# First block of a fused attention and MLP kernel: V weights loaded in two halves, tile 0 multiplied by the first half early, transposes placed inside matmul groups

## Chip, cores and metric

The kernel runs on one core of one Trainium2 chip. The metric is the device time of one execution in microseconds (us), measured on the core. The profile is one execution. Its span, from the first to the last instruction, is some 1.8 us shorter than the time.

## The reference

```python
x = A_x                                             # 1 x 2048 x 1024, bf16
h = x + attention(layernorm(x), wqkv, wo)           # 32 heads of 32, causal window of 256
h2 = h + silu(layernorm(h) @ w1) @ w2               # 1024 -> 3584 -> 1024
```

The layer norm has no weights. The argument concerns only the first 512 rows: their norm, their transposition, and their V = layernorm(x) @ wqkv[:, 2048:3072].

## The kernel before

The 2048 rows are worked on in four blocks of 512, a block in four tiles of 128 rows. At the start each tile of x is loaded, normed on VectorE and turned (transposed). TensorE turns tiles 0 to 2, and ScalarE copies the result out of PSUM. Tile 3 is turned by a DMA transpose from SBUF to SBUF. Then each tile is multiplied by the V weights in two groups of eight matmuls: `v_group(0, j, c)` is tile j times columns c*512 and up, and ScalarE evicts it. Behind these eight groups come the Q and K groups, which need all four turned tiles.

```python
for queue, c0 in ((nc.sync, 0), (nc.scalar, 512)):
    queue.dma_start(out=x_ring[0][:, c0:c0 + 512], in_=x2d[0:P, c0:c0 + 512])
load_x(0, 1)
for queue, k0 in ((nc.scalar, 0), (nc.sync, 4)):
    queue.dma_start(out=wv[:, k0:k0 + 4, 0:512], in_=wqkv_v[:, k0:k0 + 4, 2 * D:2 * D + 512])
# ... cut: one activation ...
load_x(0, 2)
load_wqkv(2 * D + 512)          # second V weights, 1 MB, rows of 1 KB
load_x(0, 3)
load_wqkv(0)                    # first Q weights
# ... cut: identity, constants ...
for i in range(11):             # warm-up matmuls on zeros
    nc.tensor.matmul(o_ps[i % 2][:].rearrange("p a b -> p (a b)"), lhsT=warm[:, 0, 0:P], rhs=warm[:, 0, :], start=True, stop=True)
# ... cut ...
ln_first(x_ring[0], ...)        # norm of tile 0, in quarters; tile 1's first statistics go in it
turn_first(x_ring[0], lnT_b[0], 0)
# ... cut: statistics of tile 1, in quarters ...
ln_first(x_ring[1], ...)
v_group(0, 0, 0, act, turn_1)   # tile 1's eight transposes ahead of its last matmul
ln_whole(x_ring[2], st, rs, 2)
v_group(0, 1, 0, act)
ln_whole(x_ring[3], st, rs, 3)
ln_transpose(x_ring[3], lnT_b[0], 3)      # DMA transpose of tile 3
for c0 in (D, 512, D + 512):
    load_wqkv(c0)                         # other Q and K weights, on the same queue
v_group(0, 0, 1, act)
turn_first(x_ring[2], lnT_b[0], 2)
v_group(0, 1, 1, act)
v_group(0, 2, 0, act); v_group(0, 2, 1, act)
# ... cut: one activation ...
v_group(0, 3, 0, act); v_group(0, 3, 1, act)
```

The softmax here doesn't subtract the row's maximum and nothing guards it: scores larger than these inputs give would overflow.

## Time and profile before

| what | before | where it is read |
|---|---|---|
| time, median of 6 runs | 697.04 us (696.97 to 698.03) | the runs |
| first V matmul | 6.89 us | timeline |
| tile 3 landed / its statistics begin | 11.9 / 12.70 us | DMA view, timeline |
| tile 3's DMA transpose, issue to landing | 15.93 + 3.2 us | DMA view |
| first Q/K matmul | 22.68 us | timeline |

In a timeline or chain, the first number is the start in us from the span's start and the second the length. In brackets stands how long the engine was idle before, and what ended that. Engines: PE is TensorE, PEld its weight load, DVE VectorE, ACT ScalarE, SPq the queue that issues DMAs. L numbers are lines of the kernel, and the change shifts them: L203 becomes L205, L251 L253, L261 L266.

### The profile page before, as it was taken

The numbers are of one execution on the slowest core, as the hardware profiler recorded it, in microseconds if no ns is written. First come the engines' busy times: TensorE is split into PE (matmuls) and PEld (weight loads), VectorE is DVE, ScalarE is ACT, GpSimd is POOL, SyncE is SP. The second block draws the span as 40 slices with busy tenths as digits, with TensorE's granted clock in tenths as the row PEclk, the third lists the DMA queues.
The fourth block names the chain that finished last, engine by engine and source line by source line (L and its number), as shares of the span: only waits on it lengthen the run. The fifth ranks groups of instructions, "written<-read, shape, count | busy, mean of one in ns | idle before, by whom it ended". The sixth has DMA issues, their size and how long they took to land.

```text
span 695.2 us, 12339 instructions
## 1 busy us (share of the span) xinstructions
PE 690.3 (99%) x5091; PEld 331.7 (48%) x5091; DVE 289.9 (42%) x618; ACT 257.9 (37%) x328; POOL 174.6 (25%) x391
## 2 busy tenths in 40 slices
PE   8999999999999999999999999999999999999998
PEld 3444454555555555544444444444444444444445
DVE  6267646644443448544316133333133251244111
ACT  4326667777777777621310023300033100233000
POOL 1007667777777677500000000000000000000000
PEclk9999999999999999999999999999999999999999
DMA  7832241036240778980023410023300025100110
GB/s 243 256 60 70 40 93 46 17 63 189 71 128 19 215 248 274 190 312 31 31 76 100 106 38 1 1 88 72 83 1 1 13 94 91 45 1 1 30 39 24
DMA packets 76617, 60.84 MB, mean 88 GB/s; under 512 B 50320, under 2 KB 60816, under 8 KB 76560
## 3 DMA queue, kind: packets, MB, share of 16 engines
q1 hardware_dynamic: 75888, 59.39, 31.2%
q8 instruction: 40, 0.66, 0.4%
q10 hardware_dynamic: 672, 0.66, 0.3%
q14 instruction: 17, 0.14, 0.1%
HBM read 39.85 MB, written 8.39 MB: 69 GB/s over the span
## 4 chain that ended last, share of the span: by engine, by line
PE 98%; DVE 1%; DMA 0%; ACT 0%; issue 0%
PE hacc L581 19%; PE hacc L618 17%; PE acc L261 16%; PE acc L618 10%; PE acc L581 9%; PE acc L251 8%; PE acc L280 7%; PE o_ps L352 4%; PE sc L298 3%; PE hacc L280 1%; PE o_ps L367 1%; PE sc L326 1%; DMA r_o<-in_A_x_dram 0%; PE tp L229 0%; DVE r_o L199 0%; DVE ln_st L171 0%
## 5 line engine op out<-in xcount | busy, mean ns | idle before, releaser
L343 POOL TENSOR_SCALAR_AFFINE_SELECT r_e<-r_e 128x256 bf16<-128x256 bf16 (+1 forms) x384 | 171.6, 477 | 116.0 <-ACT r_e L335 64.6
L306 ACT ACTIVATE r_e<-sc 128x1024 bf16<-128x1024 f32 x144 | 139.5, 1021 | 45.1 <-PE sc L298 31.0
L618 PEld LDWEIGHTS <-r_a 128*128 128x128 bf16 x952 | 90.9, 98 | 103.0
L581 PEld LDWEIGHTS <-r_w 128*128 128x128 bf16 x896 | 87.4, 98 | 104.8
L618 PE MATMUL hacc<-r_a 128*128 128x512 bf16 (+2 forms) x616 | 122.5, 360 | 0.0
L581 PE MATMUL hacc<-r_e,r_w 128*128 128x512 bf16 x456 | 100.9, 379 | 0.0
L590 ACT ACTIVATE r_n<-hacc 128x512 f32<-128x512 f32 x30 | 17.9, 597 | 178.9 <-PE hacc L581 178.9
L618 PE MATMUL acc<-r_a 128*128 128x512 bf16 x336 | 74.0, 379 | 0.0
L261 PEld LDWEIGHTS <-r_w 128*128 128x128 bf16 x512 | 46.5, 98 | 57.0 <-issue 7.0
L263 DVE CAST r_a<-acc 128x512 bf16<-128x512 f32 x56 | 38.7, 691 | 72.4 <-PE acc L261 55.7
L261 PE MATMUL acc<-r_t,r_w 128*128 128x512 bf16 x256 | 60.0, 379 | 0.0
L261 PE MATMUL acc<-r_w 128*128 128x512 bf16 x256 | 58.2, 380 | 0.0
L280 PE MATMUL acc<-r_o,r_a 128*128 128x512 bf16 x208 | 49.4, 380 | 0.0
L581 PE MATMUL acc<-r_e,r_w 128*128 128x512 bf16 x216 | 49.1, 379 | 0.0
L352 PEld LDWEIGHTS <-r_e 128*128 128x128 bf16 x1152 | 39.6, 96 | 17.0
L335 ACT ACTIVATE r_e<-sc 128x1024 bf16<-128x1024 f32 x36 | 34.9, 1021 | 21.2 <-PE sc L326 20.1
L352 PE MATMUL o_ps<-r_a,r_e 128*128 128x33 bf16 x1152 | 40.2, 178 | 0.0
L633 DVE SCALAR_TENSOR_TENSOR r_t<-hacc,r_t 128x512 bf16<-128x512 f32 (+2 forms) x22 | 14.0, 636 | 56.8 <-PE hacc L618 56.8
L280 PEld LDWEIGHTS <-r_a 128*128 128x128 bf16 x256 | 23.1, 98 | 29.6 <-issue 5.1
L633 DVE SCALAR_TENSOR_TENSOR r_t<-acc,r_t 128x512 bf16<-128x512 f32 x12 | 8.3, 692 | 64.2 <-PE acc L618 64.2
L591 DVE SCALAR_TENSOR_TENSOR r_a<-r_n,hacc 128x512 bf16<-128x512 f32 x30 | 20.6, 688 | 33.0 <-ACT r_n L590 33.0
L581 PE MATMUL hacc<-r_a,r_w 128*128 128x512 bf16 x144 | 32.9, 379 | 0.0
(75 smaller groups left out, 477.2 us busy)
## 6 DMA issues: line engine op xcount, KB each, us to landing
r_w<-in_B_w_dram SPq DMA_DIRECT2D x8, 896.0 KB, 5.2
r_a<-in_B_w_dram SPq DMA_DIRECT2D x7, 1024.0 KB, 7.7
r_w<-in_A_wqkv_dram SPq DMA_DIRECT2D x5, 1024.0 KB, 9.4
h_dram<-r_t SPq DMA_DIRECT2D x16, 256.0 KB, 3.6
r_t<-h_dram SPq DMA_DIRECT2D x16, 256.0 KB, 2.9
out_dram<-r_t SPq DMA_DIRECT2D x31, 128.0 KB, 1.7
r_o<-in_A_x_dram SPq DMA_DIRECT2D x15, 256.0 KB, 4.1
r_e<-h_dram SPq DMA_DIRECT2D x3, 1024.0 KB, 5.6
```

Source lines behind the costliest of these rows:

```text
L251: nc.tensor.matmul(acc, lhsT=lnT_b[b % 2][:, kt, j * P:(j + 1) * P], rhs=wv[:, kt, c * 512:(c + 1) * 512], start=(kt == 0), stop=(kt == KT ...
L261: nc.tensor.matmul(acc, lhsT=wqk[:, kt, col0:col0 + P], rhs=lnT_b[b % 2][:, kt, :], start=(kt == 0), stop=(kt == KT - 1))
L263: copy(out=(qT, kT)[which][b][:, g, :], in_=acc)
L280: nc.tensor.matmul(acc, lhsT=qT[b][:, g, j * P:(j + 1) * P], rhs=wo[:, g, c * 512:(c + 1) * 512], start=(g == 0), stop=(g == G - 1))
L298: nc.tensor.matmul(sc[hh // 2][:, hh % 2, ch * P:(ch + nq) * P], lhsT=kT[t // 4][r0:r0 + DH, g, (t % 4) * P:(t % 4 + 1) * P], rhs=qT[b][r0 ...
L306: nc.scalar.activation(out=e, in_=sc[pair], func=ACT.Exp, scale=scale)
L335: nc.scalar.activation(out=e, in_=sc[pair], func=ACT.Exp, scale=scale)
L343: nc.gpsimd.affine_select(out=ap, in_=ap, pattern=[[0, 2], [0, n], [sgn, P]], compare_op=ALU.is_ge if upper else ALU.is_gt, fill=0.0, base ...
L352: nc.tensor.matmul(o_ps[pair][:, qt * 2 + hh, 0:VW], lhsT=e_of(i, kind, pair)[:, hh, ch * P:(ch + 1) * P], rhs=v[:, b * 4 + kt, g * 4 + pa ...
L581: nc.tensor.matmul(acc, lhsT=w1[:, kt, ft * P:(ft + 1) * P], rhs=ln2T[b][:, kt, :], start=(kt == 0), stop=(kt == KT - 1))
L618: nc.tensor.matmul(acc[:, 0:c1 - c0], lhsT=gT[:, ft, j * P:(j + 1) * P], rhs=w2[ft // 4][:, ft % 4, c0:c1], start=(ft == 0), stop=(ft == F ...
L633: nc.vector.scalar_tensor_tensor(out=t_out[j % 2][:, c0:c1], in0=acc[:, 0:c1 - c0], scalar=0.5, in1=t_in[j % 2][:, c0:c1], op0=ALU.mult, o ...
```

## The change

The intent is to give TensorE work while it waits for tile 1's norm. The second V weights come in two loads of 256 columns. Tile 0 is multiplied by the first 256 columns right behind its first group, and tile 1's transposes stand between those matmuls. Tile 2's transposes go inside another group. Tiles 2 and 3 are normed by one instruction each, and the first half of tile 3's statistics goes ahead of tile 2's reciprocal.

```diff
-    load_x(0, 2)
-    load_wqkv(2 * D + 512)
+    for j, c0 in ((2, 512), (3, 768)):
+        nc.sync.dma_start(out=wv[:, :, c0:c0 + 256], in_=wqkv_v[:, :, 2 * D + c0:2 * D + c0 + 256])
+        if j == 2:
+            load_x(0, 2)
     load_x(0, 3)
     load_wqkv(0)
-    for i in range(11):
+    for i in range(10):
 ... cut: ln_whole takes half_done and ahead; ln_norm of the whole tile instead of four quarters;
 ... cut: turn_first turns one pair of blocks; v_cols does a group of any width;
 ... cut: turn_at(j, when) puts tile j's pairs ahead of the matmuls numbered in when
-    v_group(0, 0, 0, act, turn_1)
-    ln_whole(x_ring[2], st, rs, 2)
+    v_group(0, 0, 0, act)
+    v_cols(0, 0, 512, 768, act, turn_at(1, (3, 5, 7)))
+    turn_first(x_ring[1], lnT_b[0], 1, 3)
+    half = small.tile([P, 2, 6], F32, name="ln_st", tag="ln_st")
+    ln_whole(x_ring[2], st, rs, 2, None, (x_ring[3], half))
     v_group(0, 1, 0, act)
-    ln_whole(x_ring[3], st, rs, 3)
+    ln_whole(x_ring[3], st, rs, 3, half)
 ... cut: DMA transpose of tile 3 and the next loads, unchanged
-    v_group(0, 0, 1, act)
-    turn_first(x_ring[2], lnT_b[0], 2)
-    v_group(0, 1, 1, act)
+    v_cols(0, 0, 768, 1024, act)
+    v_group(0, 1, 1, act, turn_at(2, (3, 4, 5, 6)))
```

More of the change, by code (lines that the diff above doesn't have):

```diff
@@ L216, in ln_quarter, with ln_whole, turn_first @@
         nc.vector.bn_stats(out=stats[:, c, :], in_=xt[:, c * 256:(c + 1) * 256])
-    def ln_whole(xt, st, rs, j):
-        ln_stats(xt, st, j)
+    def ln_whole(xt, st, rs, j, half_done=None, ahead=None):
+        ln_stats(xt, st, j, half_done)
         nc.scalar.activation(out=rs[:, j:j + 1], in_=st[:, j, 1:2], func=ACT.Sqrt, bias=eps[:], scale=1.0)
+        if ahead is not None:
+            ln_half(*ahead, 0)
         nc.vector.reciprocal(out=rs[:, j:j + 1], in_=rs[:, j:j + 1])
-        for h in range(4):
-            ln_norm(xt[:, h * 256:(h + 1) * 256], st, rs, j)
-    def turn_first(xt, dst, j):
-        for h in range(4):
-            for i in range(2):
-                kt = h * 2 + i
-                nc.tensor.transpose(out=tp_ps[h][:, i * P:(i + 1) * P], in_=xt[:, kt * P:(kt + 1) * P], identity=ident[:])
-            nc.scalar.copy(out=dst[:, h * 2:(h + 1) * 2, j * P:(j + 1) * P],
-                           in_=tp_ps[h][:, 0:256].rearrange("p (k q) -> p k q", q=P))
+        ln_norm(xt, st, rs, j)
+    def turn_first(xt, dst, j, h):
+        for i in range(2):
+            kt = h * 2 + i
+            nc.tensor.transpose(out=tp_ps[h][:, i * P:(i + 1) * P], in_=xt[:, kt * P:(kt + 1) * P], identity=ident[:])
+        nc.scalar.copy(out=dst[:, h * 2:(h + 1) * 2, j * P:(j + 1) * P],
+                       in_=tp_ps[h][:, 0:256].rearrange("p (k q) -> p k q", q=P))
     def ln_tiles(tag):
@@ L244, in next_acc, with v_cols @@
         return acc_banks[acc_n[0] % len(acc_banks)]
-    def v_group(b, j, c, copy, between=None):
-        acc = next_acc()
+    def v_cols(b, j, c0, c1, copy, between=None):
+        acc = next_acc()[:, 0:c1 - c0]
         for kt in range(KT):
@@ L250, in v_group @@
                 between(kt)
-            nc.tensor.matmul(acc, lhsT=lnT_b[b % 2][:, kt, j * P:(j + 1) * P], rhs=wv[:, kt, c * 512:(c + 1) * 512],
+            nc.tensor.matmul(acc, lhsT=lnT_b[b % 2][:, kt, j * P:(j + 1) * P], rhs=wv[:, kt, c0:c1],
                              start=(kt == 0), stop=(kt == KT - 1))
-        copy(out=v[:, b * 4 + j, c * 16:(c + 1) * 16, 0:DH], in_=acc.rearrange("p (h d) -> p h d", d=DH))
+        copy(out=v[:, b * 4 + j, c0 // DH:c1 // DH, 0:DH], in_=acc.rearrange("p (h d) -> p h d", d=DH))
+    def v_group(b, j, c, copy, between=None):
+        v_cols(b, j, c * 512, (c + 1) * 512, copy, between)
     def qk_group(b, which, g, copy, between=None):
@@ L405 @@
     ln_first(x_ring[0], st, rs, 0, halves, lambda: ln_quarter(x_ring[1], quarters, 0))
-    turn_first(x_ring[0], lnT_b[0], 0)
+    for h in range(4):
+        turn_first(x_ring[0], lnT_b[0], 0, h)
     for c in range(1, 4):
@@ L409, with turn_at, between @@
     ln_first(x_ring[1], st, rs, 1, quarters)
-    def turn_1(kt):
-        if kt == 7:
-            turn_first(x_ring[1], lnT_b[0], 1)
-    v_group(0, 0, 0, act, turn_1)
-    ln_whole(x_ring[2], st, rs, 2)
+    def turn_at(j, when):
+        def between(kt):
+            if kt in when:
+                turn_first(x_ring[j], lnT_b[0], j, when.index(kt))
+        return between
+    v_group(0, 0, 0, act)
[3 more added lines that the diff above has]
+    ln_whole(x_ring[2], st, rs, 2, None, (x_ring[3], half))
     v_group(0, 1, 0, act)
-    ln_whole(x_ring[3], st, rs, 3)
+    ln_whole(x_ring[3], st, rs, 3, half)
     ln_transpose(x_ring[3], lnT_b[0], 3)
```

## The prediction

> **What bounds the kernel now.** I read the page's busy row and chain of waits first, then the chain in order of time for the first 30 us, then the timeline of the first 36 us, and last the DMA view in narrow windows, which gives the landing of single transfers. TensorE is busy nearly throughout and the chain is its own:
>
> ```profile
> PE 690.3 (99%) x5091; PEld 331.7 (48%) x5091; DVE 289.9 (42%) x618; ACT 257.9 (37%) x328; POOL 174.6 (25%) x391
> ...
> PE 98%; DVE 1%; DMA 0%; ACT 0%; issue 0%
> ```
>
> So a change to the first block can only pay by what TensorE loses before its first Q/K matmul (22.68 us); everything behind it shifts by as much. The chain in order of time shows what is lost there (start, length, what):
>
> ```profile
> 8.36 0.17 DVE rs_a L211
> 8.53 0.03 issue
> 8.56 0.35 DVE r_o L199
> 8.91 0.05 issue
> 8.96 1.05 PE tp L229 x8
> 10.02 3.67 PE acc L251 x17
> 13.69 0.45 PE tp L229 x8
> 14.13 8.71 PE acc L251 x40
> ```
>
> The eight transposes of tile 1 take 1.05 us because each pair waits for a normed quarter; the eight of tile 2, whose data are ready, take 0.45 us. TensorE also stands idle for 0.39 us before the first. The timeline gives the rest (start, length, engine, line):
>
> ```profile
> 6.89 1.67 PE L251 MATMUL acc<-r_w 128*128 128x512 bf16 x7
> 9.59 1.28 DVE L171 BATCH_NORM_STATS2 ln_st<-r_o 128x6 f32<-128x512 bf16 x2
> 11.67 1.11 DVE L199 TENSOR_SCALAR r_o<-r_o,st_a,rs_a 128x256 bf16<-128x256 bf16 x4
> 12.70 1.28 DVE L171 BATCH_NORM_STATS2 ln_st<-r_o 128x6 f32<-128x512 bf16 x2
> 14.79 1.11 DVE L199 TENSOR_SCALAR r_o<-r_o,st_a,rs_a 128x256 bf16<-128x256 bf16 x4
> 15.93 1.34 SPq L203 DMA_TRANSPOSE r_w<-r_o  x1
> 19.22 3.14 PEld L251 LDWEIGHTS <-r_w 128*128 128x128 bf16 x16 [0.40 <-DMA r_w<-r_o]
> ```
>
> Lost time: from 6.89 to 22.68 are 15.79 us. The work in it is 64 matmuls of 512 columns at 216 ns (13.82) and 16 transposes at 56 ns (0.90), 14.72 together. So 1.07 us is lost, about 1.0 of it at tile 1. At tile 3 the weight load stands 0.40 us, but the 24 matmuls from 13.97 on keep the array until 19.15, so only about 0.1 is lost there. **The ceiling of the change is thus about 1.1 us of 697**, and tile 3's DMA transpose, landing at 19.2, lies hard behind it.
>
> Landings, as issue time plus time to landing: second quarter-load of the first V half 1.72 + 5.8 = 7.5; tile 2 2.19 + 6.0 = 8.2; second V half 2.73 + 8.4 = 11.1; tile 3 and the first Q weights from
>
> ```profile
> r_o<-in_A_x_dram SPq DMA_DIRECT2D x1, 256.0 KB, 8.7
> r_w<-in_A_wqkv_dram SPq DMA_DIRECT2D x1, 1024.0 KB, 10.5
> ```
>
> 3.21 + 8.7 = 11.9 and 4.36 + 10.5 = 14.9. They land in the order of issue, 1 MB in 2.9 us (8.2 to 11.1, about 360 GB/s).
>
> [...] 16 matmuls of 512 columns between 19.22 and 22.68 are 216 ns each, and tile 2's transposes 55 ns. [...] here the warm-up matmuls start 0.43 us apart (half speed) up to the last at about 5.80, and the matmul behind it starts at 6.09, so the release came at about 5.95. [...] the new half loads have rows of exactly 512 B, which no transfer of this size in the trace has. [...] four quarters of a norm take 1.11 us, and the later norms of a whole 128x1024 tile 0.54 to 0.58 us.
>
> **The change part by part.**
> - *One warm-up matmul less.* The array is free at 5.80 instead of 6.09; the first transpose waits for the norm that ends at 5.94. The first V matmul follows the first copy of tile 0 and the last transpose pair at 6.77, so it stays at 6.89. Worth 0.
> - *V weights 512 to 1023 as two loads, tile 2 between.* The same bytes in another order: first part 7.5 + 1.45 = 8.95, tile 2 9.7 (was 8.2), second part 11.15, tile 3 unchanged 11.9.
> - *Tile 0 times columns 512 to 767 before tile 1 is needed.* The first V group runs through and ends its streaming at 6.89 + 8 x 0.216 = 8.62. The new half group waits for its weights until 8.97: a DMA wait of 0.35 us takes the place of the one on the norm (0.39). Then 8 x 0.109 = 0.87 and the transposes 8 x 0.056 = 0.45 among them; the quarters are normed at 8.91, 9.17, 9.43, 9.68, each before its pair is due (9.30, 9.63, 9.96, 10.18). Tile 1's first group starts at 10.29. Before it started at 10.07 without the half group (0.87). Gain here 0.65.
> - *Tile 1 group, second half group, tile 1's second group with tile 2's transposes in it.* 1.73 + 0.87 + 1.73 + 0.45 puts the end at 15.07, against 15.70 before: 0.63 ahead. Tile 2 must be normed when its first pair is due at 12.89 + 0.65 = 13.54.
> - *VectorE.* Tile 2's statistics start at 9.71 instead of 9.59 (landing), aggregate done at 11.23. Then comes the first half of tile 3's statistics, ahead of tile 2's reciprocal, so it waits for tile 3's landing: 11.92 to 12.55. Reciprocal and whole norm: 12.59 to 13.35, later than now (12.78) but before 13.54. Tile 3: second half 13.37 to 14.01, aggregate 14.25, square root on ScalarE 14.29 to 14.58, reciprocal, norm 14.81 to 15.37. Now it ends at 15.90: **0.53 earlier**. The DMA transpose is issued at 15.40 and, with the same 3.27 us (15.93 to 19.2), lands at 18.67.
> - *ScalarE.* Its order puts tile 3's square root before the second half group's eviction and tile 2's copies. Eviction from 14.49, first copy 14.76 to 15.15, and with the 0.10 us from copy to matmul that tile 0 shows (6.79 to 6.89) tile 2's V groups start at 15.25, not 15.07: 0.18 us of new stall.
> - *Sum.* 15.25 + 16 x 0.216 = 18.70 for tile 3's first matmul; its data are there at 18.67. Then 16 x 0.216 = 3.45: first Q/K matmul at 22.15 instead of 22.68. **Gain 0.53 us**: 0.65 won at tile 1, 0.1 of tile 3's stall removed, 0.18 lost to the copies, the remainder rounding. Behind it the program is the same and TensorE-bound, and its loads are issued some 0.5 us earlier too. 697.03 - 0.53 = 696.5.
>
> **The rivals.**
> 1. *Tile 3's landing decides.* Its half statistics now stand before tile 2's reciprocal, so tile 2 and tile 3 both hang on the landing at 11.9. If rows of 512 B cost 10%, the two half loads take 0.3 us longer, tile 3 lands at 12.2, tile 2 is normed at 13.65, tile 3's transpose lands at 18.97 and the gain falls to about 0.23 (696.8). With 20% nothing is left (697.1). For it: the DMA engines are at 0.93 to 1.09 share all the time to 14 us, so nothing hides a slower transfer. [...]
> 2. *The whole loss is removed* because the first part lands earlier than I think and tile 3 is no limit. Then 1.07 us and 696.0. Against: bytes in the queue are the same up to tile 3, and the DMA transpose has a fixed 3.27 us; 18.67 alone keeps it at about 0.55.
> 3. [...] Then the first V group runs at half speed, 1.7 us more, of which the waits at 8.95 absorb 0.35: about 698. [...]
> 4. *The gain is given back later* by a load or mask. Against: the page shows no TensorE wait but the two of this block.
>
> **Range and chances.** The ceiling at 696.0 needs rival 2; the VectorE chain makes less than 0.65 likely. On the other side a somewhat slower first transfer takes off 0.1 to 0.3. The three runs before lie within 0.07 us, so the range is mine, not noise: 696.5, from 696.2 to 697.0. 2% is 13.9 us, more than ten times the ceiling: faster 0.01, same 0.98, slower 0.01.
>
> **What would show it right or wrong.** In the profile after: (a) first V group unbroken from about 6.89; (b) the half group starting at 8.9 to 9.1 with a wait on the V weights; more than 9.2 means slow 512 B rows; (c) tile 1's transposes in pairs within 0.11 us, no wait on the norm; (d) VectorE idle for about 0.7 us before tile 3's first half statistics, until the landing near 11.9; (e) whole norms of 0.54 to 0.58 us; (f) tile 2's V groups starting near 15.25, behind the copies; (g) DMA transpose issued near 15.4, landed near 18.7; (h) first Q/K matmul near 22.15. The prediction is wrong if (h) and the end do not shift alike, if the half group's matmuls are slower than 109 ns, or if the first V group runs at half clock.

With them go the opening sentence of rival 3, which said that the clock is released later for want of the eleventh warm-up matmul, the argument against that rival, and the last argument against rival 1. The sum came to a first Q/K matmul at 22.15 us instead of 22.68, a gain of 0.53 us, and so to 696.5 us. The spacings in it are in the trace of the kernel before: 216 ns for 512 columns and 56 ns for 128 in this block, and 109 ns for the 28 matmuls of 256 columns at L618. The "release" is the step in that trace from matmuls 0.43 us apart to 0.216.

## The result

The changed kernel takes **698.60 us** as the median of 6 runs: 697.10, 697.32, 698.42, 698.77, 698.80 and 699.03. The kernel before takes 697.04 us. The ratio is 1.0014 (95% interval 1.0001 to 1.0027). Such a ratio is the mean time of one kernel's runs over that of the other's of the same rounds, so it is not quite the ratio of the medians. The prediction was 696.5 us, from 696.2 to 697.0. The runs are slower instead of faster, and they fall into two sorts, two near 697.2 and four between 698.4 and 699.0.

The profiled run (698.80 us) is of the slow sort. In its chain in order of time (start, length, what), the part that answers to the one shown of before reads:

```profile
4.50 8.09 DMA r_o<-in_A_x_dram
12.58 0.02 issue
12.61 0.69 DVE ln_st L173
...
15.35 0.56 DVE r_o L201
15.91 0.02 issue
15.93 5.13 DMA r_w<-r_o
21.06 0.05 issue
21.10 3.63 PE acc L253 x16
24.73 5.40 PE acc L266 x25
```

Before, TensorE's own matmuls filled this stretch. Now the chain hangs on tile 3. Its load lands at 12.6 us (11.9 before). Its DMA transpose is issued at 15.93, exactly as before, but takes 5.13 us instead of 3.2. TensorE then does tile 3's 16 matmuls from 21.10 instead of 19.22. TensorE's waits in the changed kernel (us in total, times, longest):

```profile
PE acc L253 <- DMA r_w<-r_o: 1.8, 1, 1.8
PE o_ps L169 <- DVE r_e L164: 1.6, 1, 1.6
PE acc L253 <- DMA r_w<-in_A_wqkv_dram: 0.6, 1, 0.6
```

The third line is the half group waiting for its weights, and the first is tile 3. The second, before the warm-up, is there in both kernels. The first Q/K matmul is at 24.57 us instead of 22.68. These 1.89 us answer to the 1.76 us by which this run is longer than the median of before, so all of the loss lies in the first block.

Two more readings. The windows view gives, behind the engines, the granted clock, the DMA engines' busy share and the GB/s. Before:

```profile
6.50:8.50 2.00, 2.00 (x12) 0.83 (x11) 1.60 (x6) 1.40 (x5) 0.00 (x0) 1.00 1.08 363
9.50:11.50 2.00, 2.00 (x13) 1.00 (x13) 1.60 (x5) 1.77 (x6) 0.00 (x0) 1.00 1.08 361
```

After, in the same stretches, while the half loads run:

```profile
6.50:8.50 2.00, 2.00 (x14) 1.01 (x13) 1.60 (x6) 1.46 (x5) 0.00 (x0) 1.00 1.17 313
9.50:11.50 2.00, 2.00 (x20) 1.55 (x20) 1.54 (x4) 1.43 (x5) 0.00 (x0) 1.00 1.18 310
```

The DMA engines are busier and move 14% less. And in the timeline, VectorE and then TensorE wait for what comes late:

```profile
12.61 0.69 DVE L173 BATCH_NORM_STATS2 ln_st<-r_o 128x6 f32<-128x512 bf16 x1 [0.95 <-DMA r_o<-in_A_x_dram]
...
14.00 0.11 PEld L231 LDWEIGHTS <-r_o 128*128 128x128 bf16 x2 [0.33 <-DVE r_o L201]
...
15.70 0.11 PEld L253 LDWEIGHTS <-r_w 128*128 128x128 bf16 x2 [0.50 <-ACT r_w L232]
```

VectorE stands 0.95 us for tile 3's landing with tile 2's reciprocal queued behind it. So the weight load stands 0.33 us before tile 2's transposes and 0.50 us before its V groups. These are not yet losses of the array, which still has matmuls queued: by the starts of the matmuls it loses less than 0.03 us at the first and 0.17 us at the second.

**What is between the transpose and its landing?** The DMA view of 18.9 to 20 us of the changed kernel shows, beside the data queue, one packet of another queue:

```profile
q1 hardware_dynamic: 209, 0.21, 80.9%
q8 instruction: 1, 0.02, 5.2%
```

The page of either kernel lists 40 such packets, 0.66 MB, so 16 KB each. Whose instructions they bring the page does not say, but the trace of the changed kernel lets one count: from the start of one such packet to the start of the next, TensorE starts 188 to 320 instructions (matmuls and weight loads), 256 in the median and 255.9 in the mean, while the medians of VectorE, ScalarE and GpSimd are 14, 16 and 18. So I take the queue q8 to bring TensorE's instructions, some 256 a packet. Whether this costs anything here is what the experiments ask.

The packet records of the trace give the times. The first fetch starts at 19.01 us and takes 0.92 us. The transpose's 1024 data packets end at 19.02. Of the 32 packets of 4 bytes behind them (semaphore updates, I think; the records do not name them), 30 end by 18.70, and the last two start at 19.92 and 19.93, when the fetch is nearly over. In the kernel before, the last of the 32 ends at 18.71, and the first fetch starts only at 23.95 us.

### The profile page after: what moved, and what is told of

It is laid out like the page before. It is cut to its first block, busy times and chain, and to the rows that moved or that the text cites. A ratio compares the mean times of both kernels' runs of the same rounds, so it can differ in the third digit from the quotient of the medians.

```text
span 697.0 us, 12347 instructions
## 1 busy us (share of the span) xinstructions
PE 690.2 (99%) x5098; PEld 332.2 (48%) x5098; DVE 288.9 (41%) x612; ACT 258.3 (37%) x329; POOL 175.2 (25%) x391
## 4 chain that ended last, share of the span: by engine, by line
PE 97%; DMA 2%; SPq 0%; DVE 0%; issue 0%; ACT 0%
PE hacc L628 21%; PE hacc L591 18%; PE acc L266 16%; PE acc L591 10%; PE acc L628 7%; PE acc L285 7%; PE acc L253 7%; PE o_ps L357 4%; PE sc L303 3%; PE hacc L285 1%; PE o_ps L372 1%; DMA r_o<-in_A_x_dram 1%; PE sc L331 1%; DMA r_w<-r_o 1%; SPq L138 0%; DVE ln_st L173 0%
## 5 line engine op out<-in xcount | busy, mean ns | idle before, releaser
L628 PE MATMUL hacc<-r_a 128*128 128x512 bf16 (+2 forms) x728 | 146.5, 363 | 0.0
L591 PE MATMUL hacc<-r_e,r_w 128*128 128x512 bf16 x432 | 95.7, 379 | 0.0
L600 ACT ACTIVATE r_n<-hacc 128x512 f32<-128x512 f32 x27 | 16.1, 597 | 175.5 <-PE hacc L591 175.5
L591 PE MATMUL acc<-r_e,r_w 128*128 128x512 bf16 x240 | 54.3, 379 | 0.0
L643 DVE SCALAR_TENSOR_TENSOR r_t<-hacc,r_t 128x512 bf16<-128x512 f32 (+2 forms) x26 | 16.7, 644 | 86.4 <-PE hacc L628 86.4
L628 PE MATMUL acc<-r_a 128*128 128x512 bf16 x224 | 49.0, 379 | 0.0
L253 PE MATMUL acc<-r_w 128*128 128x512 bf16 (+1 forms) x136 | 30.6, 367 | 2.4 <-DMA r_w<-r_o 1.8
L601 DVE SCALAR_TENSOR_TENSOR r_a<-r_n,hacc 128x512 bf16<-128x512 f32 x27 | 18.6, 688 | 29.9 <-ACT r_n L600 29.9
```

The costliest lines, as they stand in the source:

```text
L253: nc.tensor.matmul(acc, lhsT=lnT_b[b % 2][:, kt, j * P:(j + 1) * P], rhs=wv[:, kt, c0:c1], start=(kt == 0), stop=(kt == KT - 1))
L591: nc.tensor.matmul(acc, lhsT=w1[:, kt, ft * P:(ft + 1) * P], rhs=ln2T[b][:, kt, :], start=(kt == 0), stop=(kt == KT - 1))
L601: nc.vector.scalar_tensor_tensor(out=gT[:, ft, :], in0=th, scalar=1.0, in1=acc, op0=ALU.add, op1=ALU.mult)
L628: nc.tensor.matmul(acc[:, 0:c1 - c0], lhsT=gT[:, ft, j * P:(j + 1) * P], rhs=w2[ft // 4][:, ft % 4, c0:c1], start=(ft == 0), stop=(ft == F ...
```

## The experiments

**Theory 1.** More TensorE instructions now stand ahead of tile 3's matmuls: 180 against 166, since the two half groups add 16 and the warm-up loses 2. Before, so the theory goes, TensorE could not get far enough to ask for its next block before tile 3 had landed, because it was waiting for tile 3. Now it asks before, the fetch falls on the transpose, and one of the 16 DMA engines finishes its part about a microsecond late. **Theory 2** (for the missing gain in the good runs): rows of 512 B are slow to load, so the half group and tile 3 come late. **Rivals:** the slow half loads or the new order of loads make the slow runs too; or the missing warm-up matmul does, through a late clock.

Four kernels ran on one chip in each call, and "before" is the kernel before on the same chip: medians 697.00 (9 runs, 696.90 to 697.08), 696.96 (11 runs, 696.87 to 699.31) and 697.00 (9 runs, 696.90 to 697.79) in the first, second and third call.

### 1. The kernel before with 14 more TensorE instructions

```diff
-    for i in range(11):
-        nc.tensor.matmul(o_ps[i % 2][:].rearrange("p a b -> p (a b)"), lhsT=warm[:, 0, 0:P], rhs=warm[:, 0, :], start=True, stop=True)
+    for i, n in enumerate([512] * 8 + [154] * 10):
+        nc.tensor.matmul(o_ps[i % 2][:].rearrange("p a b -> p (a b)")[:, 0:n], lhsT=warm[:, 0, 0:P], rhs=warm[:, 0, 0:n], start=True, stop=True)
```

> The kernel before with only its warm-up cut otherwise: 8 matmuls of 512 columns and 10 of 154 instead of 11 of 512, the same columns and so the same time on the array, but 14 more TensorE instructions ahead of tile 3's matmuls, as the change has. Theory 1 (TensorE's first instruction fetch, a 16 KB packet, now falls on tile 3's DMA transpose because more TensorE instructions stand before it): the fetch moves from 23.95 us to about 19 us, tile 3's transpose takes up to 5 us instead of 3.2, and most runs take 698 to 699 us. Rival (the slower half loads, or the order of the loads, make the slow runs): nothing changes, 697.0 us, fetch without effect.

Measured: 698.27 to 698.78 us in five runs, median 698.43, ratio 1.0021 (1.0007 to 1.0035); none of the nine runs of before on the same chip was above 697.08. The chain:

```profile
16.04 5.01 DMA r_w<-r_o
21.10 3.63 PE acc L251 x16
24.73 5.39 PE acc L261 x25
```

The fetch starts at 18.91 us instead of 23.95 and takes 0.92 us. By the packet records no data packet of the transpose starts between 18.90 and 19.81; then ten more follow, up to 20.14. Nothing else was changed, neither a load nor a norm nor a V group. Theory 1 holds in that the fetch moved and made the loss, and the rival that needs the half loads falls for this size of loss.

### 2. The kernel before with 42 more

```diff
-    for i in range(11):
-        nc.tensor.matmul(...)
+    for i, n in enumerate([512] * 4 + [128] * 28):
+        nc.tensor.matmul(...)   # n columns, as in 1
```

> The kernel before with its warm-up in 4 matmuls of 512 columns and 28 of 128: the same columns, 42 more TensorE instructions early instead of 14. Theory (what matters is whether the first TensorE instruction fetch is asked for before tile 3's transpose lands and close to it): the fetch now comes near 15.3 us, before the transpose's packets at 17.2, the transpose takes 3.2 us again and the time is 697.0 to 697.2, although three times as many instructions were added as in the run that took 698.4. Rival (more instructions, or small warm-up matmuls, cost time as such): 698.4 or more.

Measured: 696.81 to 697.15 us, median 696.92. The fetch starts at 14.78 us and is over at 15.88, before the transpose's first packet at 17.26, and the DMA view gives the transpose 3.2 us:

```profile
r_w<-r_o SPq DMA_TRANSPOSE x1, 3.2
```

Three times as many added instructions cost nothing. It is the time of the fetch that counts, not the instructions themselves.

### 3. The changed kernel with 42 more

```diff
-    for i in range(10):
-        nc.tensor.matmul(...)
+    for i, n in enumerate([512] * 3 + [128] * 28):
+        nc.tensor.matmul(...)
```

> The changed kernel with its warm-up in 3 matmuls of 512 columns and 28 of 128, the same columns, 42 more TensorE instructions early. Theory 1: the first fetch comes some 4 us earlier, about 15 us, ahead of the transpose; the transpose takes 3.2 us again in every run and the time is 697.0 to 697.3 with no run above 697.6. Rival: still 698 to 699 in most runs.

Measured: 696.95, 697.14, 697.37, 697.44 and 698.22 us, median 697.37. In the profile the fetch starts at 15.31 and the transpose takes 3.2 us. The bulk is as expected, but one run of five is above the 697.6 that I had named. It was not profiled. The fetch is ahead of the transpose in the profiled run, so this slow run hints at a second cause (below).

### 4. The changed kernel, tile 3 turned by TensorE

```diff
-    ln_transpose(x_ring[3], lnT_b[0], 3)
-    v_group(0, 2, 1, act)
+    v_group(0, 2, 1, act, turn_at(3, (4, 5, 6, 7)))
```

> The changed kernel with tile 3 turned by TensorE inside tile 2's second V group instead of by the DMA transpose. All theories that put the slow runs on the landing of that transpose expect no slow runs; eight more transposes cost 0.45 us on TensorE, so 697.2 to 697.6 us in every run. If the slow runs stay, their cause is not that landing.

Measured: 697.43 to 697.71 us, median 697.54. No slow run in five, as expected if what the fetch delays is the DMA transpose. But the time stays 0.5 us above that of before, about the 0.45 us expected for the eight transposes.

### 5. The kernel before, only the load split in columns

```diff
-    load_wqkv(2 * D + 512)
+    for c0 in (512, 768):
+        nc.sync.dma_start(out=wv[:, :, c0:c0 + 256], in_=wqkv_v[:, :, 2 * D + c0:2 * D + c0 + 256])
```

> The kernel before with only the load of the second V half split in two of 256 columns (rows of 512 B), order unchanged. If rows of 512 B are slower, tile 3 lands at about 12.6 us instead of 11.9 and the first Q weights about 15.5; if the changed order or the queue's issue made it late, tile 3 stays at 11.9. VectorE begins tile 3's statistics at 12.70 anyway, so the time stays at 697.0 either way.

Measured: median 697.00 us (696.86 to 697.31), no change. Tile 3's load, issued at 4.40 us, takes 8.1 us in the DMA view:

```profile
r_o<-in_A_x_dram SPq DMA_DIRECT2D x1, 256.0 KB, 8.1
```

It lands at 12.5 us instead of 11.9 with the order of loads unchanged. Measured from landing to landing, the 1 MB took 3.54 us (8.23 to 11.77) against 3.00 in the kernel before (8.18 to 11.18). So rows of 512 B cost about 0.55 us for 1 MB, and theory 2 has its size. All profiles agree: a 512 KB load in rows of 512 B takes 1.75 to 1.79 us from the landing before it, and one in rows of 1 KB (runs 10 to 12, and half of the 3.00) 1.48 to 1.51. Here the time does not show it, since VectorE does not come to tile 3 before 12.74 anyway.

### 6. The changed kernel, tile 3 loaded earlier

```diff
         if j == 2:
             load_x(0, 2)
-    load_x(0, 3)
+            load_x(0, 3)
```

> The changed kernel with tile 3's load ahead of the second half of the second V weights instead of behind it. Theory (the gain is lost because tile 3 lands at 12.6 us and VectorE waits for it before it can norm tile 2): tile 3 lands near 10.9, the wait of 0.95 us on VectorE, the 0.33 us before tile 2's transposes and the 0.66 us before tile 2's V groups go, tile 3's transpose is issued near 15.1 and lands near 18.4, ahead of the first instruction fetch; first Q/K matmul near 22.05 us and 696.4 us in nearly all runs. Rival (the slow runs come from the half loads as such, or the landing does not matter): 697.1 to 698.8 as the changed kernel.

Measured: median 696.99 us (696.75 to 697.20, six runs), ratio 0.9996 (0.9984 to 1.0008). No run of the six is slow: the transpose is issued at 15.00 instead of 15.93, and its data packets are through at 17.76 when the fetch starts at 17.83. But 696.4 was not reached. TensorE waits until 9.63 us for the first half weights (0.74 us in the trace), and from there to the first Q/K matmul at 22.75 it has one wait over 0.1 us (0.13 us at 12.8, for the second half weights). Tile 3 costs it nothing here, and still nothing is gained. The first half of theory 2, the late half weights, was thus worth more than I had thought when I wrote the expectation.

### 7. The changed kernel, tile 3's statistics not ahead

```diff
-    ln_whole(x_ring[2], st, rs, 2, None, (x_ring[3], half))
+    ln_whole(x_ring[2], st, rs, 2)
-    ln_whole(x_ring[3], st, rs, 3, half)
+    ln_whole(x_ring[3], st, rs, 3)
```

> The changed kernel without the first half of tile 3's statistics ahead of tile 2's reciprocal; loads as in the change. Theory: tile 2 is normed near 12.7 us instead of 13.95 and no longer waits for tile 3's landing; tile 3's transpose is issued near 15.4 instead of 15.93, TensorE loses no 0.33 us before tile 2's transposes, first Q/K matmul near 22.2, and 696.5 us in most runs. Rival (that order on VectorE costs nothing): as the changed kernel.

Measured: 696.46, 696.57, 696.75 and 698.11, 698.32, 698.33 us. The three good runs are what theory 2 expects, 0.4 us below the runs of before. They are 0.3 us below the good runs of run 8 on the same chip, which have the half statistics ahead (and an eleventh warm-up matmul), so with late loads that order did cost about 0.3 us. The slow runs are not settled. The profiled one is slow, yet its fetch (19.78 us) follows the transpose's last data packet (19.77), and TensorE does not wait for tile 3. Instead, tile 1 came late at the very start:

```profile
1.26 4.89 DMA r_o<-in_A_x_dram
6.15 0.03 issue
6.17 0.43 DVE ln_st L218
```

Tile 1 took 4.89 us to land against 3.3 in the kernel before. VectorE takes the first quarter of tile 1's statistics ahead of tile 0's reciprocal, so tile 0's norm came late too, and TensorE stood idle before tile 0's transposes:

```profile
7.10 1.17 PE L231 MATMUL tp<-ident,r_o 128*128 128x128 bf16 x8 [1.10 <-DVE r_o L201]
8.06 3.53 PE L253 MATMUL acc<-r_w 128*128 128x512 bf16 x11
```

This shifts the first V matmul by 1.1 us (8.06 against 6.95). More is lost by the pace of the matmuls: the first seven matmuls of that group start 0.43 us apart up to 10.62, at the half speed of the warm-up, instead of 0.216, which makes 1.3 us. The mean clock listed for this run is 1.000 all the same. In this profile, then, something like rival 3 of the prediction happened. Whether an eleventh warm-up matmul would have helped this kernel was not tested.

### 8. The changed kernel with the eleventh warm-up matmul

```diff
-    for i in range(10):
+    for i in range(11):
```

> The changed kernel with the eleventh warm-up matmul put back, so 2 more TensorE instructions. Theory: no change of the good runs (the array waits for the norm anyway); the fetch comes at the same time or a little earlier and still meets the transpose, so most runs 698 to 699. If the missing warm-up matmul were the cause of the slow runs by a late clock, all runs would be 697.3 or less.

Measured: 696.82, 696.93, 696.99 and 698.75, 699.16, 699.36 us. The slow runs stay, so the missing warm-up matmul alone is not their cause. The profiled run is a good one (696.99), and it shows what the changed kernel does when the fetch does not interfere: the transpose is issued at 15.92, its data packets end at 18.72, the fetch starts at 18.73, 8 ns behind them, and the transpose lands after 3.3 us. The first Q/K matmul is at 22.76, where before has 22.68. In the profile of the changed kernel the fetch started 4 ns before the last data packet ended. So the two come so close in this kernel that a run can fall either way; the slow runs of run 8 themselves were not profiled.

### 9. The kernel before, only the whole norms

```diff
-        for h in range(4):
-            ln_norm(xt[:, h * 256:(h + 1) * 256], st, rs, j)
+        ln_norm(xt, st, rs, j)
```

> The kernel before with only the norms of tiles 2 and 3 as one instruction each. VectorE saves 0.57 us at each, tile 3's transpose is issued near 14.85 and lands near 18.1; TensorE was held by it for 0.1 us only, so 696.9 us; if the whole norm slowed another step, 697.0 or more.

Measured: 696.77, 696.90, 696.97, 697.06 and 697.87 us, median 696.97. Within noise of before and of the 0.1 us expected; inconclusive. The profile fell on the 697.87 us run, in which the first V weights landed late and held TensorE for 1.7 us, so the landing at 18.1 us could not be checked.

### 10 to 12. A split by matrix rows

If the loss is rows of 512 B and the fetch, then splitting the weights the other way avoids both. The first part is blocks 0 to 3 of the 1024 matrix rows with all 512 columns, in rows of 1 KB. Tile 0 times these stays open in its PSUM bank, and blocks 4 to 7 are added later. This needs 16 TensorE instructions fewer than the change, so 164 stand ahead of tile 3.

```diff
-    for j, c0 in ((2, 512), (3, 768)):
-        nc.sync.dma_start(out=wv[:, :, c0:c0 + 256], in_=wqkv_v[:, :, 2 * D + c0:2 * D + c0 + 256])
+    for j, k0 in ((2, 0), (3, 4)):
+        nc.sync.dma_start(out=wv[:, k0:k0 + 4, 512:1024], in_=wqkv_v[:, k0:k0 + 4, 2 * D + 512:2 * D + 1024])
-    v_cols(0, 0, 512, 768, act, turn_at(1, (3, 5, 7)))
-    turn_first(x_ring[1], lnT_b[0], 1, 3)
+    open_acc = next_acc()
+    def v_open(k0, turn=None):
+        for kt in range(k0, k0 + 4):
+            if turn:
+                turn(kt)
+            nc.tensor.matmul(open_acc, lhsT=lnT_b[0][:, kt, 0:P], rhs=wv[:, kt, 512:1024], start=(kt == 0), stop=(kt == KT - 1))
+    v_open(0, turn_at(1, (0, 1, 2, 3)))
-    v_cols(0, 0, 768, 1024, act)
+    v_open(4)
+    act(out=v[:, 0, 16:32, 0:DH], in_=open_acc.rearrange("p (h d) -> p h d", d=DH))
+    next_acc()
```

Run 10 is this alone:

> The changed kernel with the second V weights split by rows of the matrix instead of by columns: first the first four 128-row blocks with all 512 columns (rows of 1 KB), then the other four. Tile 0 is multiplied by the first four blocks where the half group stood, the sum stays open in its PSUM bank, and the other four follow after tile 1's group: 16 TensorE instructions fewer than the change, and no row of 512 B. Theory: the first part lands near 9.0 us instead of 9.44, tile 3 near 11.9 instead of 12.6, tile 3's matmuls stand at the same place in TensorE's stream as before, so the fetch falls behind the transpose; transpose issued near 15.4, first Q/K matmul near 22.1, 696.4 to 696.6 in nearly all runs. Rival (the gain is bound elsewhere): 697.0.

Run 11 adds the edit of run 7:

> The run with the split by matrix rows, and tile 3's half statistics back behind tile 2's norm. Theory: transpose issued near 15.0 instead of 15.4, no wait before tile 2's V groups; TensorE then is held by the weights near 9.0 only: 696.3 to 696.5.

Run 12 adds the edit of run 6 instead:

> The run with the split by matrix rows, and tile 3's load ahead of the second part of the weights. Theory: tile 3 lands near 10.5, transpose issued near 14.7; the second part lands near 11.9 and is wanted at 12.0, so 696.3 to 696.5; if it comes later, TensorE waits there and the gain shrinks by as much.

| run | us, five runs | median | ratio to before |
|---|---|---|---|
| 10 | 696.41, 696.54, 696.74, 696.92, 698.66 | 696.74 | 0.9999 (0.9987 to 1.0012) |
| 11 | 696.28, 696.54, 696.55, 696.66, 697.27 | 696.55 | 0.9994 (0.9981 to 1.0006) |
| 12 | 696.48, 696.58, 696.65, 696.85, 696.88 | 696.65 | 0.9994 (0.9982 to 1.0007) |

All of run 12 and four of five of run 11 lie below the fastest of the nine runs of before on that chip (696.90). The gain of some 0.4 us is what the change was after, though the interval of the ratio still takes in 1. The chain of run 11 now ends in TensorE:

```profile
15.15 7.34 PE acc L253 x34
22.49 7.55 PE acc L266 x35
```

Tile 3 costs it no wait any more, and the first Q/K matmul comes at 22.32 us (22.24 in run 12). The fetch starts at 22.56, well behind the transpose. Still, the first part lands at 9.42, not at the 9.0 expected, so 0.2 us less is gained than hoped. Its own load is as fast as thought (1.48 us); the first V weights ahead of it landed late, at 7.93 instead of 7.49. The slow run of run 10, which is the profiled one, is again of another kind: the fetch is at 24.02, but the first V weights held TensorE for 0.89 us, and the first V group then ran 3.25 us instead of 1.89, for a part at half speed (its weight loads 0.43 us apart), with a mean granted clock of 0.998 over the span.

## Why the prediction was wrong

**The step that failed** is the sentence "The DMA transpose is issued at 15.40 and, with the same 3.27 us (15.93 to 19.2), lands at 18.67". Both halves failed, for different reasons. In the good runs, where the fetch does not interfere, an earlier sentence failed as well and mattered more: "The new half group waits for its weights until 8.97".

*The 3.27 us.* In the profiled run of the changed kernel it is 5.13 us. That this comes from where TensorE's first instruction fetch falls is shown by runs 1 and 2: 14 more instructions in the kernel before make 698.43, 42 more make 696.92, with the array's work the same. My rival 2 called the transpose's time "fixed". The page had the 40 packets of the instruction queue, and I left them out. I had also noted a wait of 0.40 us at tile 3, without asking what this wait kept TensorE from doing: while it waited there at instruction 167, it could not, I think, ask for the next block. No run tests this last step alone. In keeping with it, in the six profiles with 164 or 166 instructions ahead the first fetch starts 3.9 to 4.8 us after the transpose's landing, and in the seven with 180 or more (run 4 has no such transpose) it starts before that landing.

By what mechanism one packet holds the whole is not shown. What the trace shows is that a small part comes late: the last two of the 32 4-byte packets started at 19.92, at the end of the fetch, and of the 16 semaphore updates by which the transpose lands, 15 come at 19.41 to 19.50 and the last at 21.06. In the kernel before all 16 come at 19.00 to 19.17. The trace does not explain that the landing is put at 21.06, 1.1 us after the last 4-byte packet (0.9 us in run 1), against 0.46 us (18.71 to 19.17) in the kernel before. That part is open.

*The 15.40.* It is 15.93, because tile 3 landed at 12.6 instead of 11.9. This is rival 1, and its mechanism was right: tile 3's half statistics stand ahead of tile 2's reciprocal, so both tiles hang on that landing. The term that was mis-sized is the load of rows of 512 B. I gave it 0 in the sum and 0.3 us in the rival, and it measured 0.55 us for 1 MB from landing to landing (run 5). The other 0.15 us of tile 3's 0.7 are from the loads ahead, which landed later in this profile (the first V weights were complete at 7.65 us against 7.49).

*The 8.97.* The half weights landed at 9.39 us and the half group started at 9.44, for the same reasons: 0.30 us from the rows, 0.15 from the loads ahead. This is what left the good runs without a gain. The starts of the matmuls, each gap less the 216, 109 or 56 ns of its kind, give what the array lost from its first V matmul to its first Q/K matmul:

| lost, us | at tile 1 or the half group | at the copies | at tile 3 | in all |
|---|---|---|---|---|
| before | 0.99 | 0 | 0.07 | 1.07 |
| predicted | 0.35 | 0.18 | 0 | 0.53 |
| run 8, good run | 0.76 | 0.17 | 0.13 | 1.08 |

So of the 0.53 us forecast, 0.41 went at the half group, and tile 3's landing took only 0.13. The 0.18 at the copies was right. The first Q/K matmul of that run is at 22.76, so even without the fetch no gain is left.

**The other steps, by the letters of the prediction.**
- (a) and (c) were right: the first V group is unbroken from 6.95, and tile 1's transposes come in pairs without a wait for the norm. One warm-up matmul less is worth nothing in the good runs (run 8).
- (b) was wrong, on the side I had named as the mark of slow rows: the half group starts at 9.44, not 8.97. So the 0.65 us expected at tile 1 shrinks by about as much, to 0.2.
- (d) was right in kind: VectorE waits 0.95 us, until 12.61.
- (e) was right: the whole norms take 0.55 us.
- (f) was right in kind, by ScalarE's order as worked out: tile 2's V groups start at 15.70 instead of 15.25, late as VectorE was late. The array lost 0.17 us there, as the 0.18 forecast.
- (g) and (h) were wrong, as told.

The rival of the clock (3) does not explain the loss with the fetch: in the profiles of the changed kernel and of run 1 the matmuls of the first V group start 0.216 us apart. It cannot be dismissed for the other slow runs. The mean clock listed for a run does not settle it, as run 7's profile shows (1.000, with a first group at half speed); run 10's, also at half speed for a part, lists 0.998. An idle TensorE is not enough to bring it about: in run 9's profile it stood 1.68 us for the first V weights and then went on at 0.216 us.

**What stays open.** Besides the fetch there is a disturbance at the start that no edit here controls: in the profiles of runs 7, 9 and 10 tile 1 or the first V weights land late (tile 1 took 4.89 us in run 7 against 3.3 in the kernel before, the ScalarE queue's half of the first V weights 7.4 us in run 9 against 4.8, and in run 10 the first V weights held TensorE for 0.89 us), and in two of the three a first V group at half speed (0.43 us apart) comes on top. The kernel before has slow runs too (698.03 and 699.31 us), but these were not profiled. Only one run of each kernel is profiled, so I cannot say how many of the four slow runs of the changed kernel, or of the three each of runs 7 and 8, are of which kind. That the fetch alone makes such a loss is shown in run 1. That it made the one in the profile of the changed kernel is read from the order of its packets.

## What to carry to other kernels

When a change adds instructions ahead of a short, critical DMA, look at where the engine's instruction fetches fall in the DMA view before and after: here one 16 KB packet of 0.92 us that met a DMA transpose (5.0 us instead of 3.2) cost 1.4 us (run 1: 698.43 against 697.00), more than the 1.1 us that the change could gain. Where a load can be split either way, keep its rows long: here 512 KB took 1.49 us in rows of 1 KB and 1.76 in rows of 512 B, and the split by matrix rows with an open PSUM sum did the same work. Before moving an instruction ahead of another on one engine, ask which transfer it waits for: here tile 2's reciprocal stood 0.95 us behind tile 3's statistics. And when runs of one kernel fall into sorts, look at the spacing of the first matmuls too, since the mean clock of a run can hide a slow first group (run 7's profile lists 1.000, with its first seven V matmuls 0.43 us apart).
